# Cosine attention and a GELU layer on one core: row sums of eleven quads moved from TensorE to VectorE and GpSimd

## The chip, the cores and the metric

The kernel runs on one core of a Trainium2 chip. The metric is device time in microseconds, the median of three runs.

## What is computed

Inputs q, k, v have 8 batches, 12 heads, 448 positions and 64 features per head. Rows of q and k are divided by their norm, the scores are divided by tau = 0.1, and a softmax weights v. The heads side by side form x (3584 rows of 768), which goes through a GELU layer of width 2048:

```python
q_n = q / (np.linalg.norm(q, axis=-1, keepdims=True) + 1e-06)
k_n = k / (np.linalg.norm(k, axis=-1, keepdims=True) + 1e-06)
scores = np.matmul(q_n, k_n.transpose(0, 1, 3, 2)) / tau
scores = scores - np.max(scores, axis=-1, keepdims=True)
attn = np.exp(scores)
attn = attn / (np.sum(attn, axis=-1, keepdims=True) + 1e-09)
x = np.matmul(attn, v)                 # then heads side by side
h = x @ w_in
g = 0.5 * h * (1.0 + erf(h / np.sqrt(2.0)))
out = g @ w_out
```

The kernel leaves out the subtraction of the maximum: its scores lie between -10 and 10.

## The kernel before

The order of work on each engine is written out by hand: instructions enter each engine's queue in program order, and an engine that waits holds all that is queued behind it.

Four heads make a quad; a batch has three quads, called first, second and third here (g0, g0 + 1, g0 + 2 in the code). The 448 keys of a head are cut into seven chunks of 64. One pass (`visit`) takes one chunk of a quad: `scores` issues four matmuls into a pair of PSUM banks (line 246), and `exps` lets ScalarE take the exponential of the pair into a tile `pt` in SBUF (line 253). There are three pairs of banks, numbered 0 to 2, and two single banks (`mm_tile`), used in turn.

When the seven chunks of a quad are there, `both` does the rest. `sums` adds the probabilities over all keys on TensorE with a matrix of ones: 16 matmuls (line 275). On VectorE `turned` transposes the sums (line 297), `inverted` finishes them with four small reduces across partitions (line 309) and one more, and takes the reciprocal, and `spread` transposes back twice (line 318). `values` multiplies the probabilities with v on TensorE: 28 matmuls (line 289) into a pair of banks. `normalise` multiplies with the reciprocals on VectorE into x (line 323), twice.

The norms of q and k for later quads are prepared meanwhile: `square` on GpSimd (line 156), `reduce` on VectorE (line 165), `logs` and `roots` on ScalarE (a logarithm and an exponential instead of a root), `inverses` with se on GpSimd (line 190) and rn on VectorE (line 192), `scale` on GpSimd (line 208), and `transposes`, a DMA from the sync queue that gives qkT (line 220). `upto(f, n)` runs step f for all units before n that are not done yet.

A batch runs in two stages. `attention(b, fill)` does the batch's passes and quads; between them `run()` puts in as many matmuls of the output layer of an earlier batch (line 352, 16 to an output tile, copied out by VectorE in line 356) as the next entry of `parts` says. There are 96 such fill matmuls for an odd batch and 128 for an even one. `first(b)` is the w_in stage: 96 matmuls (line 664) and 16 GELUs on ScalarE (line 701). It starts with four of the six slices of x for six output blocks, so the third quad's two slices are needed only after 24 matmuls. Two passes of the next batch stand at the end of `attention` from batch 2 on.

At the end of the w_in stage ScalarE loads its table for exponentials and does the logarithm and root for two quads of the next batch; the scaling of these quads on GpSimd follows in the next `attention`.

Of the kernel before, what the change touches and what calls it, by code (L numbers as in the profile page):

```python
# [9 lines left out]
F32 = mybir.dt.float32  # L10
BF16 = mybir.dt.bfloat16
AF = mybir.ActivationFunctionType
ALU = mybir.AluOpType
# [3 lines left out]
def kernel(  # L17
# [17 lines left out]
    nc = tc.nc  # L35
    B, H, S, D = q.shape
    C = S // D
    NQ = H // 4
# [6 lines left out]
    NB = S // 32  # L45
# [7 lines left out]
    nrm = ctx.enter_context(tc.tile_pool(name="nrm", bufs=3))  # L53
    qkbp = ctx.enter_context(tc.tile_pool(name="qkbp", bufs=3))
    qkTp = ctx.enter_context(tc.tile_pool(name="qkTp", bufs=3))
    ptp = ctx.enter_context(tc.tile_pool(name="ptp", bufs=15))
    rcp = ctx.enter_context(tc.tile_pool(name="rcp", bufs=2))
    xp = ctx.enter_context(tc.tile_pool(name="xp", bufs=1))
    gp = ctx.enter_context(tc.tile_pool(name="gp", bufs=1))
    op_ = ctx.enter_context(tc.tile_pool(name="otp", bufs=3))  # L60
# [108 lines left out]
    def logs(n):  # L169
        nq = nq_t.pop(n)  # L170
        ln_t[n] = nrm.tile(list(nq.shape), F32, tag="lq", name=f"lq{n}")
        nc.scalar.activation(ln_t[n], nq, AF.Ln, bias=tiny)
# [56 lines left out]
        rows = slice(64 * s0, 64 * s1)  # L229
        nc.vector.tensor_copy(qkT_t[g][rows, i], tp_t.pop((u, i))[rows])  # L230

    st_t = {}

    st_turn = [0]

# [12 lines left out]
        st_t[g, banks[0]] = st  # L248

    def exps(g, banks):  # L250
        st, m = st_t.pop((g, banks[0])), len(banks)
        pt = ptp.tile([128, 2, S], BF16, tag="pt", name=f"pt{g}_{banks[0][1]}")
        nc.scalar.activation(pt[:, :m], st[:, :m, :S], AF.Exp, scale=inv_tau)  # L253
        for n, (s, c) in enumerate(banks):
            pt_t[g, s, c] = pt[:, n]

    bank_t = {}

# [19 lines left out]
    def values(g, chunks=range(C), p=None):  # L278
        for c in chunks:
            if c == 0 and g < NQ:  # L280
                bank_t[g, 0] = ps_acc.tile([128, 512], F32, tag="o", name=f"o{g}_0")
                bank_t[g, 1] = mm_tile(f"o{g}_1")
            elif c == 0:
                o = pair(p, f"o{g}")
                bank_t[g, 0], bank_t[g, 1] = o[:, 0], o[:, 1]
            for s in range(2):
                for h in range(2):
                    rows, cols = slice(64 * h, 64 * (h + 1)), slice(64 * s, 64 * (s + 1))
                    nc.tensor.matmul(bank_t[g, h][cols, :S], lhsT=v_t[g][rows, s, c, :],  # L289
                                     rhs=pt_t[g, s, c][rows], start=(c == 0), stop=(c == C - 1),  # L290
                                     tile_position=(64 * h, 64 * s))
# [1 line left out]
    rs_t = {}  # L293

    def turned(g):
        tr = rcp.tile([128, NB, 32], F32, tag="tr", name=f"tr{g}")
        nc.vector.transpose(tr.rearrange("p b r -> p (b r)"), bank_t.pop((g, "sm"))[:, :S])  # L297
        bank_t[g, "tr"] = tr.rearrange("p b (k r) -> p k b r", k=2)

# [16 lines left out]
    def spread(g, h):  # L316
        rs = rcp.tile([128, NB, 32], F32, tag=f"rs{h}", name=f"rs{g}_{h}")
        nc.vector.transpose(rs, bank_t[g, "rc"][:, h].to_broadcast([128, NB, 32]))  # L318
        rs_t[g, h] = rs.rearrange("p b r -> p (b r)")

    def normalise(g, h):
        b, n = divmod(g, NQ)
        nc.vector.tensor_tensor(x_t[b][:, 2 * n + h, :], bank_t.pop((g, h))[:, :S], rs_t.pop((g, h)), ALU.mult)  # L323

    def both(g, p):
        sums(g)
        turned(g)
        inverted(g)
        spread(g, 0)
        spread(g, 1)  # L330
        values(g, p=p)
        normalise(g, 0)
        normalise(g, 1)

    ot_t = {}

# [61 lines left out]
    done = {}  # L398

    def upto(f, n, last=None):  # L400
        last = {load_qk: NG, load_v: NV, root: len(groups), load_wi: NQ + 1, load_wo: 4}.get(f, NU)
        while done.get(f, 0) < min(n, last):
            done[f] = done.get(f, 0) + 1
            f(done[f] - 1)
# [188 lines left out]
    def visit(b, pairs):  # L593
        for p in pairs:
            n, c = passes[at.get(b, 0)]
            at[b] = at.get(b, 0) + 1
            scores(b * NQ + n, ((0, c), (1, c)), p)
            exps(b * NQ + n, ((0, c), (1, c)))

    def attention(b, fill):  # L600
        fill = list(fill)
        if len(fill) == 128:
            parts = iter((20, 18, 20, 22, 32, 16))
        else:
            parts = iter((20, 13, 14, 17, 16, 16) if b == 1 else (16, 14, 16, 18, 16, 16))

        def run():
            for _ in range(next(parts)):
                fill.pop(0)()

        x_t[b] = xp.tile([128, KD, S], BF16, tag="x", name=f"x{b}")
        g0, u = b * NQ, b * NQ + 1
        run()
        upto(scale, u + 3)
        upto(transposes, u + 3)
        if b == 1:
            upto(load_qk, g0 + NQ + 2)
            upto(square, u + 4)
        visit(b, (0, 1, 2))
        if b > 1:  # L620
            upto(scale, u + 4)
            upto(transposes, u + 4)
        run()
        visit(b, (0, 1, 2))
        run()
        upto(load_qk, g0 + NQ + 3)
        visit(b, (0, 1) if b <= 2 else (0, 1, 2))
        upto(square, u + 5)
        run()
        visit(b, (0, 1, 2))  # L630
        both(g0, 0)
        upto(load_v, b + 3)
        upto(load_qk, g0 + NQ + 4)
        visit(b, (1, 2))
        upto(reduce, u + 4 + (b > 1))
        run()
        visit(b, (1, 2, 0))
        both(g0 + 1, 1)
        visit(b, (2, 0))
        n = 2 * b + 4 + (b > 1)  # L640
        if n < len(groups):
            logs(n)
            roots(n)
        run()
        both(g0 + 2, 2)
        if n < len(groups):
            inverses(n)
            done[root] = n + 1
            if b > 1:
                visit(b + 1, (0, 1))  # L650

    def first(b):
        sb, hf = divmod(b, 2)
        if hf == 0:
            g_t[sb] = gp.tile([128, KF, 2 * S], BF16, tag="g", name=f"g{sb}")
        nc.scalar.preload_act_table_set(GELU_SET)
        u = (b + 1) * NQ + 1
        hps = {}
        pairs = ({0: 1, 2: 0, 6: 1, 8: 0}, {2: 0, 4: 1, 6: 2, 8: 0}, {2: 0, 4: 1})[min(b, 2)]
        ahead = 6 if b else 5  # L660

        def mm(m, kds):
            for kd in kds:
                nc.tensor.matmul(hps[m], lhsT=wi[:, kd, m * 128:(m + 1) * 128],  # L664
                                 rhs=x_t[b][:, kd, :], start=(kd == 0), stop=(kd == KD - 1))

        def bank(m):
            if m in pairs:
                st = pair(pairs[m], f"hp{b}_{m}")
                hps[m], hps[m + 1] = st[:, 0, :S], st[:, 1, :S]  # L670
            elif m not in hps:
                hps[m] = mm_tile(f"hp{b}_{m}")[:, :S]

        for m in range(ahead):
            bank(m)
            mm(m, range(KD - 2))
        if b == 0:
            upto(square, u + 3)
            upto(scale, u + 1)
            upto(transposes, u + 1)  # L680
            upto(load_wo, 4)
            upto(reduce, u + 3)
        else:
            late = int(b == 1)
            upto(scale, u + 2 - late)
            upto(transposes, u + 2 - late)
            upto(load_qk, (b + 1) * NQ + 5)
            upto(square, u + 4 - late)
            upto(reduce, u + 4 - 2 * late)
        for m in range(ahead):  # L690
            mm(m, range(KD - 2, KD))
        for m in range(KF):
            if b == 0 and m == 8:
                for i in range(2):
                    transposes(4, i)
                    copies(4, i)
            if m >= ahead and (m == 0 or m - 1 not in pairs):
                for k in range(m, m + 1 + (m in pairs)):
                    bank(k)
                    mm(k, range(KD))  # L700
            nc.scalar.activation(g_t[sb][:, m, hf * S:(hf + 1) * S], hps.pop(m), AF.Gelu)  # L701
            if b <= 1 and m == 5:
                nc.scalar.preload_act_table_set(EXP_SET)
                upto(root, 6 if b == 0 else 8)
                nc.scalar.preload_act_table_set(GELU_SET)
                upto(scale, u + 2)
                upto(transposes, u + 2)
                if b == 0:
                    upto(load_qk, 2 * NQ + 1)
                else:  # L710
                    upto(square, u + 4)
                    upto(reduce, u + 4)
        if b + 1 < B:
            nc.scalar.preload_act_table_set(EXP_SET)
            if b <= 1:
                visit(b + 1, (0, 1, 2))
            upto(root, 2 * b + 6 + (b > 0))
# [63 lines left out]
```

## Time and profile before

| what | value |
|---|---|
| median of three runs | 414.63 us |
| the runs | 414.52, 414.63, 421.7 us |
| profiled execution, its span (the page gives no other time for it) | 412.7 us |
| TensorE (PE) busy | 406.2 us, 98% |
| ScalarE (ACT) busy | 248.4 us, 60% |
| VectorE (DVE) busy | 188.4 us, 46% |
| GpSimd (POOL) busy | 167.5 us, 41% |
| row sums (line 275), 21 quads, 0.78 us each on the chain | 4% of the span |

Busy shares are averages over the whole span; the slices and the timeline tell where an engine is full. The chain that ended last is followed back from the last instruction, and its pieces are given in order of time. In a group's line the numbers after the bar are the busy time in us and the mean duration in ns; after the second bar stands the idle time of the engine before these instructions, and what ended it.

### The profile page before, as it was taken

Reading aid. Unit: us, or ns where it says so; the run is one execution under the profiler, and the core shown is the slowest. Engines: PE = TensorE matmul, PEld = TensorE weight load, DVE = VectorE, ACT = ScalarE, POOL = GpSimd, SP = SyncE. Lnnn points to the kernel's source line nnn. Section 1 sums busy time; section 2 is a strip of 40 time slices with the busy share of each in tenths; the row PEclk is TensorE's granted clock in tenths of the full one; section 3 lists DMA queues with packets and bytes.
Section 4 is the critical chain, followed back from the end, with each engine's and each line's share of the span. In section 5 each row is a group of like instructions: output and inputs, shape, how many; then the busy total and the mean of one; then the engine's idle time right before and its main releaser. Section 6 shows DMA issues by size and latency. Waiting matters only on the chain.

```text
span 412.7 us, 8268 instructions
## 1 busy us (share of the span) xinstructions
PE 406.2 (98%) x3503; PEld 211.9 (51%) x3503; DVE 188.4 (46%) x379; ACT 248.4 (60%) x362; POOL 167.5 (41%) x115
## 2 busy tenths in 40 slices
PE   7999999999999999999999999999999999999996
PEld 3445545554555555555555555555555555555564
DVE  5786216941278222943158331773128611481021
ACT  6995686577646567664664658656665467754300
POOL 5899706084910918053730638227360233000000
PEclk9999999999999999999999999999999999999999
DMA  8999999752495507953396332965088120610033
GB/s 289 259 258 215 202 229 315 147 134 46 79 234 176 133 2 117 232 119 121 33 222 196 77 97 50 217 187 133 2 179 183 38 46 0 122 40 2 0 78 77
DMA packets 66484, 54.53 MB, mean 132 GB/s; under 512 B 38672, under 2 KB 62352, under 8 KB 66448
## 3 DMA queue, kind: packets, MB, share of 16 engines
q1 hardware_dynamic: 54464, 41.79, 39.6%
q0 software_dynamic: 11600, 11.80, 18.0%
q8 instruction: 27, 0.44, 0.4%
q10 hardware_dynamic: 384, 0.43, 0.3%
q14 instruction: 9, 0.07, 0.0%
HBM read 45.61 MB, written 11.01 MB: 137 GB/s over the span
## 4 chain that ended last, share of the span: by engine, by line
PE 85%; POOL 6%; DMA 3%; issue 2%; ACT 1%; DVE 1%; POOLq 0%; DVEq 0%
PE op L352 34%; PE hp L664 31%; PE st L246 8%; PE o L289 7%; PE sm L275 4%; DMA qkT<-qkb 3%; POOL qkb L208 2%; POOL sq L156 2%; PE op L371 1%; ACT pt L253 1%; POOL wi L387 1%; DVE nq L165 1%; POOL wo L394 0%; POOL v L141 0%; DVE rn L192 0%
## 5 line engine op out<-in xcount | busy, mean ns | idle before, releaser
L253 ACT ACTIVATE pt<-st 128x896 bf16<-128x896 f32 x168 | 142.6, 917 | 66.2 <-PE st L246 66.1
L352 PE MATMUL op<-wo,g 128*128 128x384 bf16 x864 | 147.8, 326 | 0.0
L664 PE MATMUL hp<-x,wi 128*128 128x448 bf16 x768 | 147.1, 353 | 0.0
L352 PEld LDWEIGHTS <-g 128*128 128x128 bf16 x864 | 81.5, 98 | 62.1 <-issue 10.7
L664 PEld LDWEIGHTS <-wi 128*128 128x128 bf16 x768 | 74.4, 98 | 71.6 <-issue 3.3
L701 ACT ACTIVATE g<-hp 128x448 bf16<-128x448 f32 x128 | 65.2, 546 | 67.0 <-PE hp L664 66.7
L208 POOL TENSOR_TENSOR qkb<-qk,rn 128x896 bf16<-128x896 f32 (+1 forms) x50 | 80.2, 1631 | 40.3 <-DVE rn L192 40.3
L356 DVE COPY ot<-op 128x384 f32<-128x384 f32 x54 | 29.6, 548 | 100.6 <-PE op L352 98.6
L156 POOL TENSOR_TENSOR sq<-qk 128x1792 f32<-128x1792 f32 (+1 forms) x22 | 66.6, 3038 | 13.6 <-DMA qk<-in_k_dram 13.6
L165 DVE TENSOR_REDUCE nq<-sq 128x28 f32<-128x1792 f32 (+2 forms) x30 | 48.7, 1635 | 47.9 <-POOL sq L156 44.7
L190 POOL TENSOR_SCALAR se<-sr 128x28 f32<-128x28 f32 (+1 forms) x15 | 4.5, 303 | 123.5 <-ACT sr L181 113.0
L246 PE MATMUL st<-qkT 64*64 64x448 bf16 x672 | 48.0, 358 | 0.7 <-DMA qkT<-qkb 0.5
L289 PE MATMUL o<-pt,v 64*64 64x448 bf16 x672 | 37.2, 352 | 0.0
L246 PEld LDWEIGHTS <-qkT 64*64 64x64 bf16 x672 | 18.2, 105 | 23.8 <-issue 15.1
L192 DVE RECIPROCAL rn<-se 128x28 f32<-128x28 f32 (+2 forms) x19 | 7.0, 367 | 48.7 <-POOL se L190 48.5
L318 DVE STREAM_TRANSPOSE rs<-rc 128x448 f32<-128x448 f32 x48 | 28.2, 623 | 0.8
L323 DVE TENSOR_TENSOR x<-o,rs 128x448 bf16<-128x448 f32 x48 | 27.1, 598 | 0.3
L289 PEld LDWEIGHTS <-v 64*64 64x64 bf16 x672 | 17.8, 106 | 16.7 <-issue 8.1
L297 DVE STREAM_TRANSPOSE tr<-sm 128x448 f32<-128x448 f32 x24 | 15.5, 647 | 13.4 <-PE sm L275 11.1
L275 PE MATMUL sm<-pt,ones 128*32 128x448 bf16 (+1 forms) x336 | 17.8, 332 | 0.0
L309 DVE TENSOR_REDUCE tr<-tr 32x28 f32<-32x28 f32 x84 | 16.5, 197 | 1.6
L275 PEld LDWEIGHTS <-ones 128*32 128x32 bf16 x336 | 6.8, 95 | 9.0 <-issue 7.2
(42 smaller groups left out, 120.6 us busy)
## 6 DMA issues: line engine op xcount, KB each, us to landing
qk<-in_q_dram SPq DMA_DIRECT2D x23, 448.0 KB, 6.3
qk<-in_k_dram SPq DMA_DIRECT2D x23, 448.0 KB, 8.7
out_dram<-ot SPq DMA_DIRECT2D x48, 192.0 KB, 3.6
v<-in_v_dram POOLq DMA_DIRECT2D x7, 672.0 KB, 12.4
wo<-in_moe_w_out_dram POOLq DMA_DIRECT2D x4, 768.0 KB, 13.8
wi<-in_moe_w_in_dram POOLq DMA_DIRECT2D x4, 512.0 KB, 14.3
out_dram<-ot SPq DMA_DIRECT2D x12, 96.0 KB, 2.2
wi<-in_moe_w_in_dram POOLq DMA_DIRECT2D x4, 256.0 KB, 14.3
```

Of the source, the lines that this page charges most:

```text
L156: eng.tensor_tensor(sq[:, part], t[:, part], t[:, part], ALU.mult)
L165: nc.vector.tensor_reduce(nq[:, part], sq[:, part], mybir.AxisListType.X, ALU.add)
L208: eng.tensor_tensor(qkb[:, i, :, s0:s1].rearrange("p c s d -> p s c d"), t[:, i, s0:s1], rn[:, i].to_broadcast([128, s1 - s0, C, D]), ALU. ...
L246: nc.tensor.matmul(st[cols, n, :S], lhsT=qkT[rows, 1, c, cols], rhs=qkT[rows, 0, :, cols], start=True, stop=True, tile_position=(64 * s, 6 ...
L253: nc.scalar.activation(pt[:, :m], st[:, :m, :S], AF.Exp, scale=inv_tau)
L275: nc.tensor.matmul(bank_t[g, "sm"][r:r + 32, cols], lhsT=ones, rhs=pt_t[g, s, c][:, cols], start=(c < 2), stop=(c >= C - 2), tile_position ...
L289: nc.tensor.matmul(bank_t[g, h][cols, :S], lhsT=v_t[g][rows, s, c, :], rhs=pt_t[g, s, c][rows], start=(c == 0), stop=(c == C - 1), tile_po ...
L318: nc.vector.transpose(rs, bank_t[g, "rc"][:, h].to_broadcast([128, NB, 32]))
L352: nc.tensor.matmul(ps[:, :NH], lhsT=g_t[sb][:, kf, t * 128:(t + 1) * 128], rhs=wo[:, kf, ni * NH:(ni + 1) * NH], start=(kf == 0), stop=(kf ...
L356: nc.vector.tensor_copy(ot[:, ni * NH:(ni + 1) * NH], ps[:, :NH])
L664: nc.tensor.matmul(hps[m], lhsT=wi[:, kd, m * 128:(m + 1) * 128], rhs=x_t[b][:, kd, :], start=(kd == 0), stop=(kd == KD - 1))
L701: nc.scalar.activation(g_t[sb][:, m, hf * S:(hf + 1) * S], hps.pop(m), AF.Gelu)
```

## The change

The sums of eleven quads leave TensorE. For the third quad of batches 2 to 7, `folded` adds the seven chunks on GpSimd into an f32 tile `acc`, six adds of 128 x 896. For the first quad of batches 3 to 7, all seven passes are issued before the w_in stage of the batch before, and in that stage `chunked` adds the chunks on VectorE, two reduces over a rearranged view. After either, `turned_all` and `inverted_all` do on VectorE what `turned`, `inverted` and `spread` did. The other quads keep `sums`, now called in `total`; `weighted` holds `values` and the normalising. In `attention` from batch 2 on the order of passes, quads and fill matmuls is written anew, and the w_in stage uses pairs 1 and 2 instead of 0 and 1.

The probabilities of a quad lie in one tile of seven chunks, with two such tiles, instead of fifteen tiles of one chunk each.

```diff
-    ptp = ctx.enter_context(tc.tile_pool(name="ptp", bufs=15))
-    rcp = ctx.enter_context(tc.tile_pool(name="rcp", bufs=2))
+    ptp = ctx.enter_context(tc.tile_pool(name="ptp", bufs=2))
+    rcp = ctx.enter_context(tc.tile_pool(name="rcp", bufs=1))
+    accp = ctx.enter_context(tc.tile_pool(name="accp", bufs=1))
...
+    def folded(g, chunks=range(C)):
+        for c in chunks:
+            if c == 1:
+                acc_t[g] = accp.tile([128, 2, S], F32, tag="acc", name=f"acc{g}")
+            if c:
+                nc.gpsimd.tensor_tensor(acc_t[g], all_t[g][:, 0] if c == 1 else acc_t[g], all_t[g][:, c], ALU.add)
+
+    def chunked(g, s):
+        if s == 0:
+            acc_t[g] = accp.tile([128, 2, S], F32, tag="acc", name=f"acc{g}")
+        nc.vector.tensor_reduce(acc_t[g][:, s], all_t[g][:, :, s].rearrange("p c q -> p q c"),
+                                mybir.AxisListType.X, ALU.add)
+
+    def turned_all(g):
+        tr = rcp.tile([128, 2 * NB, 32], F32, tag="tr", name=f"ta{g}")
+        nc.vector.transpose(tr.rearrange("p b r -> p (b r)"), acc_t.pop(g).rearrange("p s q -> p (s q)"))
+        su = bank_t[g, "su"] = rcp.tile([128, 2, 2, NB], F32, tag="sa", name=f"sa{g}")
+        nc.vector.tensor_reduce(su[:, 0].rearrange("p s b -> p (s b)"), tr, mybir.AxisListType.X, ALU.add)
+        for j in range(4):
+            o = j ^ 1
+            nc.vector.tensor_copy(su[32 * j:32 * (j + 1), 1], su[32 * o:32 * (o + 1), 0])
+
+    def inverted_all(g):
+        su = bank_t.pop((g, "su"))
+        s2 = rcp.tile([128, 2, NB], F32, tag="su", name=f"su{g}")
+        for s in range(2):
+            for h in range(2):
+                nc.vector.tensor_reduce(s2[64 * s:64 * (s + 1), h],
+                                        su[64 * h:64 * (h + 1), :, s].rearrange("p k b -> p b k"),
+                                        mybir.AxisListType.X, ALU.add)
+        rc = bank_t[g, "rc"] = rcp.tile([128, 2, NB], F32, tag="rc", name=f"rc{g}")
+        nc.vector.reciprocal(rc, s2)
+        spread(g, 0)
+        spread(g, 1)
...
     def attention(b, fill):
+        elif b == 2:
+            parts = iter((20, 16, 16, 16, 16, 14, 14, 16))
         else:
+            parts = iter((20, 18, 18, 18, 26, 28) if len(fill) == 128 else (14, 12, 14, 14, 20, 22))
...
         run()
         upto(scale, u + 3)
         upto(transposes, u + 3)
+        upto(scale, u + 4)
+        upto(transposes, u + 4)
...          # from batch 3 on:
+            visit(b, (1, 2))
+            weighted(g0, 0)
+            visit(b, (1, 2))
+            run()
+            upto(load_qk, g0 + NQ + 3)
+            upto(square, u + 5)
+            visit(b, (0, 1, 2))
+            upto(load_v, b + 3)
         run()
         visit(b, (0, 1, 2))
+        folded(g0 + 2, range(1) if b == 2 else range(3))
+        upto(reduce, u + 5)
         run()
         upto(load_qk, g0 + NQ + 4)
+        total(g0 + 1)
         visit(b, (1, 2))
+        weighted(g0 + 1, 0)
+        visit(b, (1, 2))
+        n = 2 * b + 5
...          # from batch 3 on:
+            folded(g0 + 2, range(3, C))
+            run()
+            if b + 1 < B:
+                visit(b + 1, (1, 2, 0))
         if n < len(groups):
             logs(n)
             roots(n)
             inverses(n)
...
+        run()
+        turned_all(g0 + 2)
+        inverted_all(g0 + 2)
+        if b + 1 < B:
+            visit(b + 1, (1, 2))
+        weighted(g0 + 2, 0)
+        if b + 1 < B:
+            visit(b + 1, range(1, 1 + C - at[b + 1]))
...
     def first(b):
-        pairs = ({0: 1, 2: 0, 6: 1, 8: 0}, {2: 0, 4: 1, 6: 2, 8: 0}, {2: 0, 4: 1})[min(b, 2)]
+        pairs = ({0: 1, 2: 0, 6: 1, 8: 0}, {2: 0, 4: 1, 6: 2, 8: 0}, {2: 1, 4: 2})[min(b, 2)]
...
             upto(square, u + 4 - late)
+            if 1 < b < B - 1:
+                chunked((b + 1) * NQ, 0)
+                chunked((b + 1) * NQ, 1)
             upto(reduce, u + 4 - 2 * late)
+            if 1 < b < B - 1:
+                turned_all((b + 1) * NQ)
+                inverted_all((b + 1) * NQ)
```

More of the change, by code (lines that the diff above doesn't have):

```diff
@@ L230, in copies @@
         nc.vector.tensor_copy(qkT_t[g][rows, i], tp_t.pop((u, i))[rows])
-    st_t = {}
+    st_t, all_t = {}, {}
     st_turn = [0]
@@ L250, in exps @@
     def exps(g, banks):
-        st, m = st_t.pop((g, banks[0])), len(banks)
-        pt = ptp.tile([128, 2, S], BF16, tag="pt", name=f"pt{g}_{banks[0][1]}")
-        nc.scalar.activation(pt[:, :m], st[:, :m, :S], AF.Exp, scale=inv_tau)
+        st = st_t.pop((g, banks[0]))
+        if g not in all_t:
+            all_t[g] = ptp.tile([128, C, 2, S], BF16, tag="pt", name=f"pt{g}")
+        (s0, c0), (s1, c1) = banks
+        pt = all_t[g][:, c0] if c0 == c1 else all_t[g][:, c0:c1 + 1, s0]
+        nc.scalar.activation(pt, st[:, :, :S], AF.Exp, scale=inv_tau)
@@ L254, in exps @@
         for n, (s, c) in enumerate(banks):
             pt_t[g, s, c] = pt[:, n]
+    acc_t = {}
+    def folded(g, chunks=range(C)):
[9 more added lines that the diff above has]
+                                mybir.AxisListType.X, ALU.add)
@@ L295, in turned @@
     def turned(g):
-        tr = rcp.tile([128, NB, 32], F32, tag="tr", name=f"tr{g}")
+        tr = rcp.tile([128, 2 * NB, 32], F32, tag="tr", name=f"tr{g}")[:, :NB]
         nc.vector.transpose(tr.rearrange("p b r -> p (b r)"), bank_t.pop((g, "sm"))[:, :S])
@@ L323, in normalise, with total @@
         nc.vector.tensor_tensor(x_t[b][:, 2 * n + h, :], bank_t.pop((g, h))[:, :S], rs_t.pop((g, h)), ALU.mult)
-    def both(g, p):
+    def total(g):
         sums(g)
@@ L330, in both, with weighted @@
         spread(g, 1)
+    def weighted(g, p):
         values(g, p=p)
@@ L333, in both @@
         normalise(g, 1)
+    def both(g, p):
+        total(g)
+        weighted(g, p)
     ot_t = {}
@@ L601, in attention, with run @@
         fill = list(fill)
-        if len(fill) == 128:
-            parts = iter((20, 18, 20, 22, 32, 16))
-        else:
-            parts = iter((20, 13, 14, 17, 16, 16) if b == 1 else (16, 14, 16, 18, 16, 16))
-        def run():
-            for _ in range(next(parts)):
+        if b == 1:
+            parts = iter((20, 13, 14, 17, 16, 16))
+        elif b == 2:
+            parts = iter((20, 16, 16, 16, 16, 14, 14, 16))
+        else:
+            parts = iter((20, 18, 18, 18, 26, 28) if len(fill) == 128 else (14, 12, 14, 14, 20, 22))
+        def run(n=None):
+            for _ in range(next(parts) if n is None else n):
                 fill.pop(0)()
@@ L618, in attention @@
             upto(square, u + 4)
[L619 to L622, printed above, removed]
+            visit(b, (0, 1, 2))
+            run()
+            visit(b, (0, 1, 2))
+            run()
+            upto(load_qk, g0 + NQ + 3)
+            visit(b, (0, 1))
+            upto(square, u + 5)
+            run()
+            visit(b, (0, 1, 2))
+            both(g0, 0)
+            upto(load_v, b + 3)
+            upto(load_qk, g0 + NQ + 4)
@@ new lines, in attention @@
+            visit(b, (1, 2))
+            upto(reduce, u + 4)
+            run()
+            visit(b, (1, 2, 0))
+            both(g0 + 1, 1)
+            visit(b, (2, 0))
+            logs(6)
+            roots(6)
+            run()
+            both(g0 + 2, 2)
+            inverses(6)
+            done[root] = 7
+            return
+        upto(scale, u + 4)
+        upto(transposes, u + 4)
+        if b == 2:
+            visit(b, (0, 1, 2))
+            run()
+            upto(load_qk, g0 + NQ + 3)
+            upto(square, u + 5)
+            visit(b, (0, 1, 2))
+            run()
+            total(g0)
+            visit(b, (1, 2))
+            weighted(g0, 0)
+            upto(load_v, b + 3)
+            visit(b, (1, 2))
+        else:
+            visit(b, (1, 2))
+            weighted(g0, 0)
+            visit(b, (1, 2))
+            run()
+            upto(load_qk, g0 + NQ + 3)
+            upto(square, u + 5)
+            visit(b, (0, 1, 2))
+            upto(load_v, b + 3)
@@ L623, in attention @@
         run()
         visit(b, (0, 1, 2))
+        folded(g0 + 2, range(1) if b == 2 else range(3))
+        upto(reduce, u + 5)
         run()
[L626 to L632, printed above, removed]
         upto(load_qk, g0 + NQ + 4)
+        total(g0 + 1)
         visit(b, (1, 2))
-        upto(reduce, u + 4 + (b > 1))
-        run()
-        visit(b, (1, 2, 0))
@@ L638, in attention @@
-        both(g0 + 1, 1)
-        visit(b, (2, 0))
-        n = 2 * b + 4 + (b > 1)
+        weighted(g0 + 1, 0)
+        visit(b, (1, 2))
+        n = 2 * b + 5
+        if b == 2:
+            run()
+            visit(b, (0,))
+            folded(g0 + 2, range(1, C))
+            visit(b + 1, (1, 2))
+        else:
+            folded(g0 + 2, range(3, C))
+            run()
+            if b + 1 < B:
+                visit(b + 1, (1, 2, 0))
         if n < len(groups):
@@ L643, in attention @@
             roots(n)
-        run()
-        both(g0 + 2, 2)
-        if n < len(groups):
             inverses(n)
             done[root] = n + 1
-            if b > 1:
-                visit(b + 1, (0, 1))
+        if b == 2:
+            run()
+            visit(b + 1, (0, 1, 2))
+        run()
+        turned_all(g0 + 2)
+        inverted_all(g0 + 2)
+        if b + 1 < B:
+            visit(b + 1, (1, 2))
+        weighted(g0 + 2, 0)
+        if b + 1 < B:
+            visit(b + 1, range(1, 1 + C - at[b + 1]))
+        assert not fill, len(fill)
     def first(b):
```

## The prediction

> **What bounds the kernel now.** I read the busy shares first, then the chain that ended last, then windows by stage, then queues of single engines. The page's shares and slices:
>
> ```profile
> PE 406.2 (98%) x3503; PEld 211.9 (51%) x3503; DVE 188.4 (46%) x379; ACT 248.4 (60%) x362; POOL 167.5 (41%) x115
> PE   7999999999999999999999999999999999999996
> PEclk9999999999999999999999999999999999999999
> ```
>
> TensorE is never idle after the first slice, at full clock. So an instruction taken from it is worth its whole place in the chain, and any wait put on it costs in full. The chain in batch 5 (an odd one, 96 output matmuls to fill with), in order of time; columns are start, us, what:
>
> ```profile
> 255.36 0.69 PE st L246 x12
> 256.05 3.03 PE op L352 x18
> 259.08 0.69 PE st L246 x12
> 259.77 0.78 PE sm L275 x16
> 260.55 1.45 PE o L289 x28
> 262.00 0.42 PE st L246 x8
> 262.41 2.71 PE op L352 x16
> ...
> 273.77 18.27 PE hp L664 x96
> ```
>
> One quad's row sums (sm) hold the chain for 0.78 us, its values (o) for 1.45, one pass of scores (st, four matmuls) for 0.23, one output matmul (op) for 2.71/16 = 0.169, the w_in stage for 18.27. The stage windows of batches 4 to 5 show the room on the others:
>
> ```profile
> 228.02:246.28 18.26, 18.26 (x97) 9.43 (x98) 6.81 (x8) 10.59 (x18) 9.59 (x4) 1.00 0.33 87
> 246.28:273.77 27.49, 27.49 (x314) 14.23 (x312) 15.28 (x36) 19.11 (x26) 11.21 (x8) 1.00 0.68 161
> ```
>
> After the span the columns are PE, PEld, DVE, ACT, POOL. VectorE is busy 6.8 of 18.3 us in the w_in stage: it has 11.5 us free there. Last, what follows a w_in stage (ending at 246.28), from the timelines of ScalarE, VectorE, GpSimd and the sync queue:
>
> ```profile
> 248.18 0.34 ACT L172 ACTIVATE lq<-nq,tiny 128x56 f32<-128x56 f32 x1
> 249.33 0.50 DVE L192 RECIPROCAL rn<-se 128x56 f32<-128x56 f32 x1 [6.75 <-POOL se L190]
> 249.91 6.62 POOL L208 TENSOR_TENSOR qkb<-qk,rn 128x896 bf16<-128x896 f32 x4 [0.62 <-DVE rn L192]
> 256.50 3.17 POOL L156 TENSOR_TENSOR sq<-qk 128x1792 f32<-128x1792 f32 x1
> 253.27 4.83 SPq L220 DMA_TRANSPOSE qkT<-qkb  x2
> 264.89 2.00 DVE L165 TENSOR_REDUCE nq<-sq 128x28 f32<-128x1792 f32 x1
> ```
>
> GpSimd starts to scale 3.63 us after the stage's end (once rn is done), the third quad's transpose is issued at +7.0 and lands 4.0 later (the median of these transfers), at +11.0, the square ends at +13.4, and its reduce runs only at +18.6. Before, nobody needs these early.
>
> **What is removed.** Eleven quads lose their sums on TensorE: the third of batches 2 to 7, the first of 3 to 7. 11 x 0.78 = 8.6 us, all on the chain. This is the whole gain; without any new wait the time would be 406.0.
>
> **What is added on GpSimd.** Six adds of 128x896 per third quad. The nearest rows are L208 (1.69 us for 896) and L156 (3.17 for 1792): between 1.6 and 1.7 each, 10 us per batch, issued after the square and the 0.9 us v load. In an odd batch they end near 3.63 + 9.75 + 0.9 + 10 = 24.3 us after the stage, or 28.9 with the late start found below. I cost them at nothing: turned_all stands on VectorE behind the copy of the last output tile, which TensorE finishes at 23.8 without and at 31.4 with that delay, and turned_all's own cover is the next item. At 2.3 us per add that cover would be gone, and each further 0.1 us would cost 0.6 in such a batch. Behind the adds in GpSimd's queue stand se, the scaling of the next second quad and two squares (9.6 us busy in the w_in window above); the first of their users is the norm reduce 16 us into the next w_in stage, so they have room. What follows that copy is a serial chain: copy 0.56, hand-off 0.06, a 128x896 transpose (twice L297's 448 less one fixed part) 1.1, reduce of 896 (L165) 1.08, four 32-row copies and four reduces at 0.2 (L309) 1.6, reciprocal 0.33, two spreads 1.17, two normalises 1.12: 7.0 us. The w_in stage can run 24 of its matmuls (4.57) before it needs the third quad's x; with the values and two to four score passes the cover is 6.9 us in batches 3 to 6, 6.5 in batch 2, 6.0 in batch 7. Stalls 0.1 x 4 + 0.5 + 0.95 = 1.85 us; with the small ones at 0.1 instead of 0.2 nearly none, at 0.3 some 6.5.
>
> **What is moved on the scores.** Two passes, values (1.45), two passes: the last of them writes the pair of banks that the second exponential reads. That one ends 2.10 us after the group began (0.37 to the first start, as 249.25 against 248.88 in batch 5, and 1.73 for two); TensorE is there at 0.46 + 1.45 + 0.23 = 2.14. The hand-back is between 0 and the 0.14 of the hand-over; I take 0.10, so 0.06 over: 15 such places, 0.9 us (0 to 1.5). The probabilities now lie in two tiles of a whole quad instead of fifteen of a chunk; the exponentials of a quad wait for the values of the quad two before, which stand ahead of them on TensorE each time: nothing. Loads on the sync queue keep their order but for two stores.
>
> **What is added on VectorE, and decides.** Two reduces per first quad, each over 3136 bf16 elements per partition whose innermost step is 1792 bytes. No row has such a step at length. The rows at hand (line, operation, count, busy, mean ns):
>
> ```profile
> L165 DVE TENSOR_REDUCE nq<-sq 128x28 f32<-128x1792 f32 x20 | 40.1, 2007 | 44.7 <-POOL sq L156 44.7
> L165 DVE TENSOR_REDUCE nq<-sq 128x14 f32<-128x896 f32 x6 | 6.3, 1078 | 0.4 <-ACT sq L154 0.3
> L188 DVE TENSOR_REDUCE se<-root 128x14 f32<-128x28 f32 x2 | 0.4, 178 | 0.1
> L309 DVE TENSOR_REDUCE tr<-tr x84: 189/197/207, 67.4 to 370.0; 32x28 f32<-32x28 f32 x84
> ```
>
> Contiguous input goes at (2007 - 1078)/896 = 1.04 ns per element over a fixed 150 ns, which the 178 ns for 28 elements confirms. L309 reads its 28 elements 64 bytes apart and takes 189/197/207 (shortest, median, longest): 1.39, 1.68 or 2.04 ns per element. One chunked reduce is then 3.4 us (contiguous), 4.5, 5.4 or 6.55. L309 is the nearest, being the only reduce that jumps; since a short one can hide some of its first reads in the fixed part, I take midway between median and longest, 1.86 ns, 6.0 us, and keep 3.4 and 6.55 as ends.
>
> [...]
>
> Now the queue. The normalises end 4.6 us into w_in; behind them stand two chunked reduces, two norm reduces (4.05), turned_all and inverted_all (1.1 + 1.08 + 1.6 + 0.33 + 1.17 = 5.28), and only then rn. They end at 4.6 + 12.0 + 4.05 + 5.28 - 18.27 = 7.6 us after the stage, rn at 8.1, and GpSimd starts at 8.2 instead of 3.63. What is late next: the first quad's normalises, the third quad's qkT (start + 7.36), which the change scores after only 40 fill matmuls, and the square with its reduce (start + 9.75 + 2.02), behind which an output copy (0.55) must free the PSUM tile that the second quad's sums take. The logarithm lq is 0.5 us late as well, since the norm reduces end at +2.4; the exponentials queued behind it lie inside the same stalls. The sums decide: start + 12.33 = 20.5 us. TensorE would be at those sums after 54 fills, 10 passes and one values block, 9.14 + 2.3 + 1.45 = 12.9 us in odd batches, and after 74 fills at 16.3 in even ones. Stall 7.6 in batches 3 and 5, 4.3 in 4 and 6. Batch 7 has one norm reduce less ahead and no square: start 6.2, qkT at 13.5 against 9.8 (40 fills, 7 passes, values): 3.7. Together 15.3 + 8.5 + 3.7 = 27.5 us.
>
> **Sum.** -8.6 + 27.5 + 1.85 + 0.9 = +21.7 on the span of 412.7, the only time the page gives for that execution: 434.4. The median of the runs, 414.63, lies 1.9 above it: 436.3 us. By L309's median it is 430.7, by its longest 442.0, by its shortest 421.9.
>
> **Rivals.** (1) The strided reduce runs at the contiguous rate. Then VectorE is done 2.5 us after the stage, rn stays where it is (3.55), and three stalls remain that the price does not touch: 3.63 + 12.33 - 12.9 = 3.1 in batches 3 and 5, qkT 11.0 against 9.8 in batch 7. -8.6 + 6.1 + 1.2 + 2.75 = +1.5: 416.1, no slower by a measurable amount. For it: the linear 1.04 over three sizes; against it: 197 for 178 in L309, though its 18 ns could be a fixed price of reading other partitions than it writes. It turns to slower by 2% from about 4.7 us per reduce. (2) All is hidden: norms and transposes come early enough and 406.0 results, just over 2% faster. Against it: the 3.1 us above follows from rows of before alone. (3) The stalls also drop the clock, or further queues block: 447 and more. PEclk shows 9 in all slices, but with no gap as long as the 3 to 4 us expected here.
>
> **Chances.** Forecast 0.62, rival 1 0.26, rival 2 0.05, rival 3 0.07. The forecast's own range is 421 to 447; taking in rival 1, 412 to 447. About 2% is what a measurement of this kernel can tell from no change: faster 0.05, same 0.29 (rival 1 and the forecast's low end), slower 0.66.
>
> **What would show it.** Right: the chunked reduces at 5.4 to 6.6 us; VectorE above 9 tenths in w_in stages from batch 2 on; rn and the qkb scaling 7 to 9 us after each of those stages; TensorE waiting for x's normalise, qkT and, last, the sums' PSUM tile. Wrong: reduces near 3.4 us and TensorE idle only about 3 us in batches 3 and 5. If the copy-to-normalise chain takes over 8 us, w_in waits in each batch, and the steps on the tail were mis-sized.

## The result, and the profile after

The changed kernel takes 459.68 us (median of four, 457.58 to 460.56) against 414.8 before: 1.108 times as long, interval 1.105 to 1.111. One of the four runs before took 421.7 us, in a slower state that the ratio leaves out. Slower was forecast, with 436.3 and a range of 421 to 447; the measured time lies 13 us above it. The profiled execution took 459.56 with a span of 457.8.

Busy shares and slices of the kernel after:

```profile
PE 413.0 (90%) x3327; PEld 213.2 (47%) x3327; DVE 288.4 (63%) x433; ACT 248.9 (54%) x362; POOL 235.4 (51%) x151
PE   7999999999994989959989599795998989799996
DVE  5775039515669956699565995659966499255012
PEclk9999999999997998989999799997999999899999
```

TensorE has 176 matmuls fewer and is now idle in notches from slice 13 on; its granted clock, 1.000 over the span of before, is 0.966 over this one and falls behind the deeper ones. VectorE gained 100 us of busy time. What TensorE waited for, from the list of waits (us in total, times, longest):

```profile
PE hp L767 <- DVE x L364: 24.7, 8, 6.8
PE st L247 <- DMA qkT<-qkb: 7.6, 4, 3.0
PE sm L316 <- DVE ot L403: 3.5, 3, 1.8
```

The last two are waits that the forecast rested on. The first stands in the middle of the w_in stage, where TensorE waits for the third quad's normalised x (line 364 here is `normalise`); it was expected at 1.85 us. One such place, batch 4 into its w_in stage, from the timelines of TensorE, VectorE and GpSimd (start, us):

```profile
249.23 4.71 PE L767 MATMUL hp<-x,wi 128*128 128x448 bf16 x24
258.59 3.68 PE L767 MATMUL hp<-x,wi 128*128 128x448 bf16 x9 [4.64 <-DVE x L364]
```
```profile
248.42 1.08 DVE L280 TENSOR_REDUCE sa<-ta 128x28 f32<-128x896 f32 x1
249.54 6.13 DVE L283 COPY sa<-sa 32x28 f32<-32x28 f32 x4
255.71 0.75 DVE L290 TENSOR_REDUCE su<-sa 64x14 f32<-64x28 f32 x4
```
```profile
245.66 3.33 POOL L209 TENSOR_TENSOR qkb<-qk,rn 128x896 bf16<-128x896 f32 x2 [0.45 <-DVE rn L193]
248.95 6.30 POOL L157 TENSOR_TENSOR sq<-qk 128x1792 f32<-128x1792 f32 x2
```

Four copies of 28 elements on 32 partitions take 6.1 us. They end at 255.7; GpSimd's two squares end at 255.25. One copy takes up to 3.12 us; the first three of batch 2 (0.41, 3.12 and 3.10 us) each end within 0.04 us of the end of a GpSimd instruction, and the fourth, with GpSimd idle, takes 0.17. How long the four take goes by what GpSimd still has to do: 6.1 to 6.9 us in batches 2 to 5 beside two squares, 3.19 in batch 6 beside one, 0.74 in batch 7 beside none:

```profile
364.66 3.19 DVE L283 COPY sa<-sa 32x28 f32<-32x28 f32 x4
364.07 3.17 POOL L157 TENSOR_TENSOR sq<-qk 128x1792 f32<-128x1792 f32 x1
415.62 0.74 DVE L283 COPY sa<-sa 32x28 f32<-32x28 f32 x4
```

For the first quads, whose copies come just after a w_in stage with GpSimd idle or nearly so, the four take 0.77 (217.80, first quad of batch 4). Behind the wait at 258.59 the first nine matmuls take 0.41 us each, where the 24 before the wait took 0.20: the granted clock is 0.50 from 258.59 to 262.27, and was 1.00 from 249.23 to 253.94.

The operations that the prediction priced, by shape (count, busy us, mean ns; the second answer has shortest, median and longest):

```profile
L273 DVE TENSOR_REDUCE acc<-pt 128x448 f32<-128x3136 bf16 x10 | 54.9, 5528 | 0.0
L283 DVE COPY sa<-sa 32x28 f32<-32x28 f32 x44 | 33.7, 767 | 1.0
L278 DVE STREAM_TRANSPOSE ta<-acc 128x896 f32<-128x896 f32 x11 | 12.1, 1102 | 0.0
L268 POOL TENSOR_TENSOR acc<-acc,pt 128x896 f32<-128x896 f32 x30 | 56.6, 1886 | 3.7 <-ACT pt L257 1.4
```
```profile
L283 DVE COPY sa<-sa x44: 167/173/3120, 133.7 to 416.2; 32x28 f32<-32x28 f32 x44
```

### The profile page after: what moved, and what is told of

It is laid out like the page before. It is cut to its first block, busy times and chain, and to the rows that moved or that the text cites. A ratio compares the mean times of both kernels' runs of the same rounds, so it can differ in the third digit from the quotient of the medians.

```text
span 457.8 us, 8009 instructions
## 1 busy us (share of the span) xinstructions
PE 413.0 (90%) x3327; PEld 213.2 (47%) x3327; DVE 288.4 (63%) x433; ACT 248.9 (54%) x362; POOL 235.4 (51%) x151
## 4 chain that ended last, share of the span: by engine, by line
PE 36%; POOL 24%; issue 17%; DVE 14%; ACT 4%; DMA 4%; POOLq 0%; ACTq 0%; DVEq 0%
PE op L399 15%; PE hp L767 14%; POOL qkb L209 8%; POOL sq L157 7%; POOL acc L268 6%; DVE sa L283 4%; DMA qkT<-qkb 4%; PE st L247 3%; ACT pt L257 3%; DVE acc L273 2%; DVE nq L166 2%; PE sm L316 1%; DVE sa L280 1%; PE op L418 1%; DVE ta L278 1%
## 5 line engine op out<-in xcount | busy, mean ns | idle before, releaser
L767 PE MATMUL hp<-x,wi 128*128 128x448 bf16 x768 | 157.5, 366 | 24.7 <-DVE x L364 24.7
L399 PE MATMUL op<-wo,g 128*128 128x384 bf16 x864 | 150.7, 330 | 0.0
L767 PEld LDWEIGHTS <-wi 128*128 128x128 bf16 x768 | 76.5, 101 | 104.0 <-issue 40.7
L247 PE MATMUL st<-qkT 64*64 64x448 bf16 x672 | 52.2, 363 | 10.3 <-DMA qkT<-qkb 7.6
L268 POOL TENSOR_TENSOR acc<-acc,pt 128x896 f32<-128x896 f32 x30 | 56.6, 1886 | 3.7 <-ACT pt L257 1.4
L273 DVE TENSOR_REDUCE acc<-pt 128x448 f32<-128x3136 bf16 x10 | 54.9, 5528 | 0.0
L283 DVE COPY sa<-sa 32x28 f32<-32x28 f32 x44 | 33.7, 767 | 1.0
L330 PEld LDWEIGHTS <-v 64*64 64x64 bf16 x672 | 19.3, 107 | 12.7 <-issue 1.7
L268 POOL TENSOR_TENSOR acc<-pt 128x896 f32<-128x896 bf16 x6 | 11.3, 1885 | 10.9 <-ACT pt L257 10.8
```

Of the source, the lines that this page charges most:

```text
L247: nc.tensor.matmul(st[cols, n, :S], lhsT=qkT[rows, 1, c, cols], rhs=qkT[rows, 0, :, cols], start=True, stop=True, tile_position=(64 * s, 6 ...
L268: nc.gpsimd.tensor_tensor(acc_t[g], all_t[g][:, 0] if c == 1 else acc_t[g], all_t[g][:, c], ALU.add)
L273: nc.vector.tensor_reduce(acc_t[g][:, s], all_t[g][:, :, s].rearrange("p c q -> p q c"), mybir.AxisListType.X, ALU.add)
L283: nc.vector.tensor_copy(su[32 * j:32 * (j + 1), 1], su[32 * o:32 * (o + 1), 0])
L399: nc.tensor.matmul(ps[:, :NH], lhsT=g_t[sb][:, kf, t * 128:(t + 1) * 128], rhs=wo[:, kf, ni * NH:(ni + 1) * NH], start=(kf == 0), stop=(kf ...
```

## The experiments

**e1: reduces instead of the copies.** The operation changes, not the data, the partitions or the order.

```diff
-            nc.vector.tensor_copy(su[32 * j:32 * (j + 1), 1], su[32 * o:32 * (o + 1), 0])
+            nc.vector.tensor_reduce(su[32 * j:32 * (j + 1), 1],
+                                    su[32 * o:32 * (o + 1), 0].rearrange("p s (b w) -> p s b w", w=1),
+                                    mybir.AxisListType.X, ALU.add)
```

> The four 32-row copies of turned_all are replaced by reduces over an axis of length one (same elements, same partitions). Theory 1 (the copies are held while GpSimd executes): the reduces take 0.2 us each also behind a busy GpSimd, the gaps before x in the w_in stages (7.2, 5.8, 5.0, 5.8, 2.1 us) shrink to under 1 us, TensorE keeps its clock there, and the time falls from 459.7 to 425 to 432. Rival 1a (crossing partitions or reading a tile just written is what is slow): the four reduces still take 3 to 7 us and the time stays above 450.

Measured: 434.46 us, 1.0475 of before (1.0454 to 1.0495). The line and the waits:

```profile
L283 DVE TENSOR_REDUCE sa<-sa x44: 169/173/177, 134.4 to 391.9; 32x28 f32<-32x28 f32 x44
```
```profile
PE st L247 <- DMA qkT<-qkb: 12.4, 5, 3.3
PE sm L318 <- DVE ot L405: 2.3, 2, 1.2
PE st L247 <- DVE x L366: 1.7, 2, 1.0
PE hp L769 <- DVE x L366: 1.4, 4, 0.7
```

The time is 2.5 us above what theory 1 gave (the wait at qkT grew from 7.6 to 12.4), but what holds the copies does not hold the reduces: each of the 44 takes 0.17 to 0.18 us, beside the same busy GpSimd, and the wait inside w_in falls from 24.7 to 1.4 us. Crossing partitions and reading a fresh tile are not the price: rival 1a falls. The copies cost 25.2 us, slower matmuls behind the waits included. What is left is the wait list of the forecast: qkT, the sums' tile, the first normalise.

**e2: the same number of elements, read in memory order.** As e1, and:

```diff
-        nc.vector.tensor_reduce(acc_t[g][:, s], all_t[g][:, :, s].rearrange("p c q -> p q c"),
+        nc.vector.tensor_reduce(acc_t[g][:, s], all_t[g].rearrange("p c s q -> p (c s q)")[:, s * C * S:(s + 1) * C * S].rearrange("p (q c) -> p q c", c=C),
```

> As e1, and the two chunked reduces read the same number of bf16 elements in memory order (groups of seven neighbours, so the sums are not those of the keys). Theory 2 (the step of 1792 bytes costs 0.68 ns per element): 3.4 us per reduce instead of 5.5, VectorE ready about 4 us earlier after each w_in stage, waits at qkT and at the sums' tile mostly gone, 415 to 420 us. Rival 2a (bf16 input or the length is slow): 5.5 us again and the time of e1.

Measured: 418.9 us, 1.0098 (1.0081 to 1.0114).

```profile
L273 DVE TENSOR_REDUCE acc<-pt x10: 3397/3400/3406, 138.3 to 337.3; 128x448 f32<-128x3136 bf16 x10
```
```profile
PE st L247 <- DMA qkT<-qkb: 3.6, 4, 1.5
PE sm L318 <- DVE ot L405: 3.1, 2, 1.7
```

3.40 us instead of 5.53, and 15.6 us less: the step of 1792 bytes costs (5528 - 3400)/3136 = 0.68 ns per element, as theory 2 had it. Of the 15.6 us some 9.5 are waits, most of them at qkT (12.4 to 3.6). Another 5.9 are slower matmuls: the same 3327 keep TensorE busy for 405.7 us in e1 and 399.8 in e2, since in e1 the clock falls after the three waits at qkT of 2.8 to 3.3 us, and in e2 it never falls (granted 0.984 over the profile of e1, 1.0 over that of e2). The sums of e2 are not those of the keys, so it gives the price of the read and is no kernel to use.

**e3: first quads back on TensorE.** As e1, without `chunked` and what follows it in `first`, and with `total(g0)` ahead of the first passes in `attention` from batch 3 on.

> As e1, but the first quads keep their sums on TensorE (at the head of the next attention); VectorE has no chunked reduces. Theory 2 (VectorE's queue in the w_in stage delays rn): GpSimd starts to scale 3.6 us after the stage again; 0.78 x 6 = 4.7 us are gained by the third quads, 3.1 us lost at the sums' tile in batches 3 and 5, some us where GpSimd's adds end late in odd batches: 414 to 420 us. Rival 2b (the new order of passes itself delays qkT and the sums): above 425.

Measured: 422.49 us, 1.0186 (1.0163 to 1.0209), 2.5 above the expected range. Against e2, where the first quads' sums lie on VectorE at the contiguous price, it is 3.6 us slower: nearly 5 x 0.78 = 3.9. So taking these sums from TensorE would be worth about what the chain said if VectorE could take them in time; at the real price of the read it is not: e1, which has them on VectorE, is 12 us slower than e3.

**e4: the order alone.** As e3, with the third quads' sums on TensorE too: `folded`, `turned_all` and `inverted_all` are replaced by `total(g0 + 2)`.

> The new order of passes, quads and fill matmuls with all sums on TensorE as before: nothing on GpSimd or VectorE in their place. If the moved sums are what costs, 416 to 421 us: three waits of 3.1, 3.1 and 1.2 us at the sums' tile and at qkT. Rival 2b (the order costs most of the 45 us): above 430.

Measured: 426.62 us, 1.0299 (1.0229 to 1.0369): between the two expectations, a little nearer the rival's. By the medians the third quads' adds on GpSimd gain 4.1 of 6 x 0.78 = 4.7 us (e4 against e3), and the order costs 11.7 with nothing moved. These two are uncertain by some us: the four runs of e4 spread from 425.0 to 430.9, and by its two shortest the adds gain 2.7 and the order costs 10.3. Of the order's cost the list of waits shows 5.6 at one place:

```profile
PE sm L318 <- DVE ot L405: 5.6, 6, 1.8
PE st L247 <- DMA qkT<-qkb: 0.5, 1, 0.5
```

A second part is the scores. Counted from each matmul's start to the next one's, those after the first 60 us take 36.6 us in e4 and 33.1 in before, 3.5 more; inside the closer groups of passes there are 16 gaps of 0.13 us. Both profiles were granted the full clock (1.0). The rest, under 2 us, falls behind fill matmuls.

**e5 and e6: the norm reduce later.** On e3 and e4:

```diff
-        upto(reduce, u + 5)
         run()
         upto(load_qk, g0 + NQ + 4)
         total(g0 + 1)
         visit(b, (1, 2))
         weighted(g0 + 1, 0)
+        upto(reduce, u + 5)
...
-(14, 12, 14, 14, 20, 22)
+(18, 16, 17, 9, 16, 20)
```

> As e3 (first quads on TensorE, third quads on GpSimd, reduces for the copies), with the norm reduce of the attention stage moved on VectorE behind the second quad's normalising, and 11 of the odd batches' fill matmuls moved ahead of the third quad's scores. Theory 3 (in the order of the change the sums' PSUM tile waits for an output copy that is held by a reduce that waits for GpSimd's square): the waits at the sums (0.6 to 2.1 us in batches 3 to 6) and at qkT go, 422.5 falls to 414 to 417 us. Rival 3a (the copy or the sums wait for something else): 420 or more.

> As e4 (the new order, all sums on TensorE), with the same two moves as e5. Theory 3: 5.6 us of waits at the sums go, 426.6 falls to 418 to 421 us; what then stays above 414.9 is the price of the order that is not this wait. The difference to e5 is what GpSimd's adds gain: 6 x 0.78 less their tail, 3 to 4.5 us.

Measured: e5 432.25 us, 1.0451 (1.0404 to 1.0498), ten slower than e3; e6 426.37, 1.0277 (1.0263 to 1.0291), the same as e4. Both expectations fail. From the lists of waits, e5 and then e6:

```profile
PE hp L770 <- DVE x L366: 6.7, 8, 2.3
PE sm L318 <- DVE ot L405: 4.5, 5, 1.1
```
```profile
PE sm L318 <- DVE ot L405: 5.1, 7, 1.1
PE op L401 <- DVE ot L405: 1.6, 4, 0.6
```

The wait at the second quad's sums is gone in both (in e5 they start at 168.08 with none). But the sums of the first quad stand right behind the first fills in e3 to e6, and now they wait in odd batches too, for the copy of an output tile that on VectorE stands behind rn (1.1 us before 156.19 in e5). And in e5 the fills that were moved forward had covered GpSimd's adds: these end at 179.8, VectorE's chain at 187.7, and the longest waits inside w_in are 1.5, 1.5 and 2.3 us in the odd batches. With two moves in one kernel, the two runs do not show what each is worth. No run removes these waits as well, so whether the third quads' gain can be had below 414.9 is not known.

**e7: adds instead of the strided reduces.** As e1, and in `chunked`:

```diff
-        nc.vector.tensor_reduce(acc_t[g][:, s], all_t[g][:, :, s].rearrange("p c q -> p q c"),
-                                mybir.AxisListType.X, ALU.add)
+        for c in range(1, 4) if s == 0 else range(4, C):
+            nc.vector.tensor_tensor(acc_t[g], all_t[g][:, 0] if c == 1 else acc_t[g], all_t[g][:, c], ALU.add)
```

> As e1, with the two strided reduces of a first quad replaced by six adds on VectorE (128 x 896, contiguous, two inputs from SBUF each; the same sums). Theory 2 (the step is the price): 6 x 1.08 = 6.5 us instead of 11.0 where GpSimd is idle, and the time near that of e2, 418 to 422 us. Theory 1 adds that an operation with two SBUF inputs may be held like the copies while GpSimd executes: then the first adds of a stage, which meet the end of GpSimd's squares, take 1 to 3 us. Rival 2c (anything that sums on VectorE there is too late): the time of e1, 434.

Measured: 424.81 us, 1.0263 (1.0220 to 1.0306), 9.7 faster than e1 and 2.8 above the expected range; all seven chunks are still added.

```profile
L274 DVE TENSOR_TENSOR acc<-acc,pt x25: 1092/1092/1094, 143.3 to 346.5; 128x896 f32<-128x896 f32 x25
L274 DVE TENSOR_TENSOR acc<-pt x5: 1072/3517/3521, 139.7 to 340.6; 128x896 f32<-128x896 bf16 x5
```
```profile
189.10 3.52 DVE L274 TENSOR_TENSOR acc<-pt 128x896 f32<-128x896 bf16 x1
192.72 5.88 DVE L274 TENSOR_TENSOR acc<-acc,pt 128x896 f32<-128x896 f32 x5
```
```profile
185.36 6.30 POOL L157 TENSOR_TENSOR sq<-qk 128x1792 f32<-128x1792 f32 x2
```

The 25 adds that meet an idle GpSimd take 1.09 us. The first of a stage, an add of the same size, meets GpSimd's last square in four of the five stages and takes 2.60 or 3.52 us there, more than the 1 to 3 expected; in the fifth it meets none and takes 1.07. In the stage shown the square ends at 191.7, and the add 1.0 later. So not only the copies are held. In both cases the hold lasted to the end of the GpSimd instruction in flight: the held copies of batch 2 in after end within 0.04 us of it, this add 1.0 us behind it, where 1.07 is its length beside none.

The steps add up (medians in us; before and e1 to e4 were measured side by side, after in a comparison of its own):

| from | to | difference |
|---|---|---|
| before, 414.9 | e4, the order alone, 426.6 | +11.7 |
| e4 | e3, third quads on GpSimd, 422.5 | -4.1 |
| e3 | e2, first quads on VectorE, read in memory order, 418.9 | -3.6 |
| e2 | e1, the strided read, 434.5 | +15.6 |
| e1 | after, copies in turned_all, 459.7 | +25.2 |

## Why the prediction was right or wrong

**Gain, right.** 8.6 us were expected of eleven sums. TensorE's busy time falls from 408.9 us in e4 to 399.8 in e2, which is that much and a little more; of the time, e4 to e3 to e2 gives 7.7 by the medians and 6.3 by e4's two shortest runs.

**VectorE's queue in the w_in stage, right in kind, too dear in size.** The forecast took 1.86 ns per element between L309's 1.68 and 2.04; measured are (5528 - 150)/3136 = 1.71, L309's median, and 1.04 in memory order. That a short reduce hides some of its first reads, the forecast's reason to go above the median, no run shows: 1.68 over 28 elements and 1.71 over 3136 are nearly the same. In e1, where no other wait hides it, GpSimd starts to scale 6.8 to 6.9 us after the stages that lead into batches 4 and 5 (210.86 against 204.0, 263.66 against 256.9); 8.2 was forecast, and the prediction's own sum gives 7.3 with 5.53 us per reduce. The waits that follow are those named, but smaller: 27.5 us were forecast, and in e1 those at qkT, at the sums and at the first normalise come to 12.4 + 2.3 + 1.7 = 16.4. The 5.9 us of slower matmuls, which the sum did not have, stand beside them.

**Rival 1's reading of L309, answered.** It held that the reduce's 197 ns, against 178 for as many elements in L188, might be the price of reading other partitions than it writes. The reduces of e1 do that with neighbouring elements and take 173 ns, so the step is the likelier price. With the read in memory order, e2, the time is 418.9; rival 1 gave 416.1, with 3.1 us at the sums in each of batches 3 and 5, where e2's list shows 3.1 for two waits together.

**The tail behind the last output copy, wrong, and it decides.** The step that failed is "four 32-row copies and four reduces at 0.2 (L309) 1.6". A copy was priced by a reduce on the same partitions. The reduces took 0.18; the copies 0.17 when GpSimd is idle and up to 3.12 each, 6.1 to 6.9 for four, when it executes. The waits inside w_in came to 24.7 us, not 1.85. The chain was 7.0 us on paper; from the last output copy to the last normalise it took 13.4, 13.4 and 12.3 us in batches 2 to 4 (130.5 to 143.9 in batch 2). The prediction listed the scaling and the squares behind GpSimd's adds and asked only who waits for them; it did not ask what they do to a VectorE that runs beside them. The bound of 0.3 us for the small ones was far too narrow. The sign that the prediction gave for this, a chain of over 8 us and a wait inside w_in in each batch, is what the profile shows.

Beside a busy GpSimd, two kinds of VectorE operation were held: the copies in after (up to 3.12 us) and the first adds in e7 (up to 3.52). The reduces in e1 (0.17) were not. Why those two and not the reduces, no run shows; nor whether GpSimd is held in turn: its adds took 1.87 to 1.90 us throughout.

That e1, with this step mended, lands at 434.5, beside the forecast's 436.3, is luck: the waits of VectorE's queue were 11 us smaller than forecast, and slower matmuls and the order's cost, mostly left out, stand in their place.

**The clock, given as part of a rival, came true.** After the four waits of 4.6 to 6.9 us in w_in, 6 to 15 matmuls ran slow, which cost 1.0 to 2.7 us each, 7.6 together. In the stages of after:

```profile
131.90:159.60 27.70, 20.85 (x100) 10.04 (x97) 27.43 (x20) 9.51 (x17) 8.39 (x4) 0.88 0.25 64
190.30:215.50 25.20, 19.79 (x101) 9.70 (x98) 24.97 (x18) 10.41 (x18) 6.96 (x3) 0.93 0.25 65
```

The last three columns are the granted clock, the DMA share and GB/s; VectorE, third after the span, is busy all through, though part of that is a copy that stands still.

**GpSimd's adds, mis-sized:** 1.89 us, not 1.6 to 1.7, six with their gaps in 11.7. In after, VectorE's chain starts 1.5 to 3.5 us after they end in batches 2 to 4, each time behind the last output copy, so little came of it; in e5 it did.

**The order, underestimated.** Three waits of 3.1, 3.1 and 1.2 us were seen from rows of before, and 0.9 for the closer passes. In e4 the sums of the second quad in batches 3 and 5 wait 1.7 and 1.8 us, and the closer passes cost 3.5; the whole is 11.7 us (10.3 by the two shortest runs). Some of its 5.6 us at sums come from its own place for the first quad's, which after does not have.

## What to carry to other kernels

Price an operation by its own kind and its neighbours, not by its size (here a copy of 28 elements took 0.17 us with GpSimd idle and up to 3.12 beside it): when work moves to GpSimd, look at every VectorE operation that will run beside it, and try a reduce where a copy between SBUF tiles would stand beside GpSimd. In e1, beside GpSimd's squares, the reduces took 0.17 us each and two normalises, which read one operand from PSUM, 1.11 together, as elsewhere. A reduce over an axis that is not innermost in memory cost 1.6 times a contiguous one here; six contiguous adds in the place of two such reduces took 7.1 us from start to end with GpSimd idle and 9.5 with the first one held, against 11.0. And when TensorE is full, an order that pulls work forward also pulls forward each wait on another engine's queue, which may cost more than what was taken away: here 11.7 us against 7.7.

## What was not expected of the hardware

A VectorE copy of 28 elements between SBUF tiles took up to 3.12 us beside GpSimd, and successive ones were held anew (0.41, 3.12 and 3.10 us in batch 2 of after). A reduce with a step of 1792 bytes cost the same per element, 1.71 ns, as L309's with 64 bytes, 1.68. The clock of TensorE fell after waits as short as 1.98 us (in batch 3 of after, 11 matmuls ran slow behind one, and the granted clock from 171.8 to 176.7 was 0.65). It stayed up in after behind waits of 1.76 us and less, and in e2, e3 and e4, whose longest waits at the sums were 1.7, 1.8 and 1.8 us and whose granted clock was 1.0. The length of the wait alone did not decide: in e7, granted 0.996 over its profile, the clock fell after one of 1.98 us, at 266.3, and stayed up after one of 2.82 us, at 166.2.
